# Tying the first feed-forward product of each token group behind attention in TensorE's queue

## The chip, the cores and the metric

The kernel runs on one core of a Trainium2 chip. The metric is the device time of one execution in microseconds (us). Its engines are TensorE (PE in the profile; PEld is its loading of weights), VectorE (DVE), ScalarE (ACT), GpSimd (POOL) and SyncE (SP, which issues the DMAs). Each engine works its own queue in order, and the queues run side by side, joined by semaphores.

## The reference

Attention, then two blocks of feed-forward layers, in fp32:

```python
# q, k, v: batch 2, heads 8, sequence 576, head size 64
q_d, k_d, v_d = mean over groups of 4 positions            # 144 positions
out_d = softmax(scale * q_d @ k_d.T) @ v_d                 # pooled attention
out_local = softmax(scale * q @ k.T where |i - j| < 4) @ v # local attention
x = repeat(out_d, 4) + out_local                           # 1152 tokens x 512
h = relu(x @ w_in); x = (s * h * h + b) @ w_out            # 512 -> 2048 -> 512
out = sum over 4 experts e of p[:, e] * (relu(x @ w1[e]) @ w2[e])   # 512 -> 1024 -> 512
```

## The kernel before

**Attention in units.** A unit is one head pair of one group of tokens. There are four groups (each of the two batch entries in two halves, of 256 and 320 tokens) with four head pairs each: 16 units, u = 0 to 15. A loop over `i` (line 979) runs a software pipeline. In iteration i it traces `b_step(i-1)` (scores: one mask product, the local score products of line 580, pooled products of line 594 or 604, then maxima on VectorE and exponentials on ScalarE), `a_step(i)` (transposes of k, line 487, for the first half of a batch entry, and of q, line 505), `k_step(i)`, `d_step(i-3)` (output products, lines 667 and 674), `c_step(i-2)` (transposes of the probabilities, line 646), `x_step(i-3)` (x of this head pair, split in a high and a low part), `norm_step(i-1)` and `v_step(i-1)`. For units 0 to 3 `keep_warm` (line 350) adds filler matmuls.

**The feed-forward products.** Each fp32 product is made of three reduced-precision ones (high times high, high times low, low times high, `PAIRS`), by the helper `products` (line 311; its matmuls are line 316). A product of the first layer contracts over four blocks of 128 rows, one for each head pair, so it is 12 matmuls, and the first three need x of head pair 0 only. The first feed-forward block (n = 0; 512 of the 2048 hidden columns) works on the attention's four token groups. For each group it has eight steps: four products of the first layer (`moe1_l1`, fc = 0 to 3; relu, square, scale and split of h behind each) and four of the second (`moe1_l2`). The weights come as halves of 256 columns, which ScalarE and VectorE reformat and split (`prep`, lines 154 to 203).

**The order.** When the last head pair of a group is done (`x_step` of u = 3, 7, 11, 15), the group's eight steps are appended to the list `slots` (line 1000). For group 0 three are taken at once; after that one is taken behind each `k_step` and each `c_step`, while there are any. So by the program the first product of group 0 stands behind `c_step(4)`, that of group 1 behind `a_step(11)` and that of group 2 behind `a_step(15)`. Group 3's steps are appended in the last iteration, and are taken in the loop of line 1018 and in the plan behind it.

This is the order of the trace, not that of the queues. The planner that makes the queues goes by the program's order as a priority, but puts an instruction ahead where, by its own estimates, the inputs are there and the engine would be free. A tile of a pool with a tag takes one of the tag's buffers when its first instruction is placed; the products' PSUM banks have the tag "m" with three buffers (pool `psm`), the attention's have five (pool `psa`).

After the attention (`actx.close()`, line 1021) all further blocks follow by a plan of due times.

Of the kernel before, what the change touches and what calls it, by code (L numbers as in the profile page):

```python
# [22 lines left out]
def attn_moe_moe_kernel(  # L23
# [14 lines left out]
    nc = tc.nc  # L38
# [11 lines left out]
    W = 72  # L50
# [6 lines left out]
    KD = DM // P  # L57
    BLK = 512
    FC = BLK // P
# [287 lines left out]
    idle = const.tile([P, 512], BF16, name="idle")  # L347
    nc.vector.memset(idle, 0.0)

    def keep_warm(ps, c0, m):  # L350
        for _ in range(m if c0 < 448 else 0):
            nc.tensor.matmul(  # L352
                ps[:, c0:], idle[:, :P], idle[:, : 512 - c0], start=True, stop=True
            )
# [122 lines left out]
    def a_step(u):  # L477
        g, j, b, hf = unit(u)
        if hf == 0:
            kn = loaded.pop(("k", u))  # L480
            kT = ap1.tile([P, S], F32, tag=f"kT{j}", name=f"kT{j}")
            view = kT.rearrange("p (n r) -> p n r", r=KR)
            m = KR // 2
            for c in range(2):
                psk = bank()
                for i in range(m):
                    nc.tensor.transpose(  # L487
                        psk[:, i * KP : i * KP + KP],
                        kn[:, c * m + i].rearrange("p a d -> p (a d)"),
                        ident[:KP, :KP],  # L490
                    )
                keep_warm(psk, m * KP, fill[u])
                nc.scalar.activation(
                    out=view[:, :, c * m : c * m + m],
                    in_=psk[:, : m * KP].rearrange("p (t n) -> p n t", n=KP),
                    func=ACTF.Copy,
                    scale=scale / (FAC * FAC),
                )
            st["kT", j] = kT
        qn = loaded.pop(("q", u))  # L500
        n0, m = tiles(hf)
        gd = m * TQ // FAC
        psq = bank()
        for r in range(FAC):
            nc.tensor.transpose(  # L505
                psq[:, r * gd : r * gd + gd],
                qn[:gd, r].rearrange("p a d -> p (a d)"),
                ident[:gd, :gd],
            )
        keep_warm(psq, m * TQ, fill[u])  # L510
        qz = ap2.tile([P, MX * TQ], F32, tag="qz", name="qz")[:, : m * TQ]
        nc.scalar.activation(
            out=qz.rearrange("p (t n r) -> p t n r", t=m, r=FAC),
            in_=psq[:, : m * TQ].rearrange("p (r t n) -> p t n r", r=FAC, t=m),
            func=ACTF.Copy,
            scale=float(FAC * FAC),
        )
        qd = ap2.tile([P, MX * TQ // FAC], F32, tag="qd", name="qd")[:, :gd]
        nc.vector.tensor_reduce(
            out=qd,  # L520
            in_=psq[:, : m * TQ].rearrange("p (r n) -> p n r", r=FAC),
            axis=AX.X,
            op=ALU.add,
        )
        st["q", u] = qz, qd
# [18 lines left out]
    def b_step(u):  # L544

        g, j, b, hf = unit(u)
        n0, m = tiles(hf)
        gd = m * TQ // FAC
        qz, qd = st.pop(("q", u))
        kT = st["kT", j]  # L550
        kd = st["kd", j]
        pl = ap2.tile([P, MX, W], F32, tag="pl", name="pl")[:, :m]
        ml = ap2.tile([P, MX, 1], F32, tag="ml", name="ml")[:, :m]
        both = gd == GB
        pd = ap2.tile([P, 2, SD], F32, tag="pd", name="pd")
        md = ap2.tile([P, 2, 1], F32, tag="md", name="md")
        if both:
            pd, md = pd[:, :1], md[:, :1]
        else:
            pd, md = pd[:gd], md[:gd]  # L560
        sm = sums[u % 2]

        def exps(out, ps, m, total):
            nc.scalar.activation(  # L564
                out=out, in_=ps, func=ACTF.Exp, bias=m, scale=1.0, accum_out=total
            )

        ps = [bank()] + ([] if both else [bank()])
        nc.tensor.matmul(  # L569
            ps[0][:, : m * W],  # L570
            identb.rearrange("p a q -> p (a q)"),
            mask[:, hf * 2 : hf * 2 + m].rearrange("p t w -> p (t w)"),
            start=True,
            stop=False,
        )
        for t in range(m):
            k0 = window(n0 + t)
            for a in range(2):
                o = slice(a * D, a * D + D)
                nc.tensor.matmul(  # L580
                    ps[0][a * TQ : a * TQ + TQ, t * W : t * W + W],
                    qz[o, t * TQ : t * TQ + TQ],
                    kT[o, k0 : k0 + W],
                    start=False,
                    stop=t == m - 1,
                )
        local = ps[0][:, : m * W].rearrange("p (t w) -> p t w", w=W)
        nc.vector.tensor_reduce(out=ml, in_=local, axis=AX.X, op=ALU.max, negate=True)
        pooled = [] if both else [ps[0][:gd, MX * W : MX * W + SD], ps[1][:gd, :SD]]
        if both:  # L590
            pooled = [ps[0][: 2 * gd, MX * W : MX * W + SD]]
            for a in range(2):
                o = slice(a * D, a * D + D)
                nc.tensor.matmul(  # L594
                    ps[0][a * gd : a * gd + gd, MX * W : MX * W + SD],
                    qd[o, :],
                    kd[o, :],
                    start=True,
                    stop=True,
                )  # L600
        else:
            for a in range(2):
                o = slice(a * D, a * D + D)
                nc.tensor.matmul(pooled[a], qd[o, :], kd[o, :], start=True, stop=True)  # L604
        for a in range(len(pooled)):
            nc.vector.tensor_reduce(
                out=md[:, a], in_=pooled[a], axis=AX.X, op=ALU.max, negate=True
            )
        for t in range(m):
            exps(pl[:, t], local[:, t], ml[:, t], sm[:, t])  # L610
        for a in range(len(pooled)):
            exps(pd[:, a], pooled[a], md[:, a], sm[: pd.shape[0], MX + a])
        st["p", u] = pl, pd
# [17 lines left out]
    def c_step(u):  # L631


        g, j, b, hf = unit(u)
        pl, pd = st.pop(("p", u))
        m, rows, n = pl.shape[1], pd.shape[0], pd.shape[1]
        pT = ap2.tile([W, (MX + MX // 2 + 1) * P], F32, tag="pT", name="pT")
        cols = [(pl[:, t], P) for t in range(m)]
        cols += [(pd[:, a, c * ND : c * ND + ND], rows) for a in range(n) for c in range(2)]
        c0 = 0  # L640
        while cols:
            ps = bank()
            n = 0
            while cols and n + cols[0][1] <= 512:
                x, width = cols.pop(0)
                nc.tensor.transpose(ps[:W, n : n + width], x, ident[:width, :width])  # L646
                n += width
            keep_warm(ps, n, fill[u])
            nc.scalar.copy(pT[:, c0 : c0 + n], ps[:W, :n])
            c0 += n  # L650
        st["pT", u] = pT

    def d_step(u):
# [8 lines left out]
        ps = bank()  # L662
        for a in range(2):
            o = slice(a * D, a * D + D)
            for c in range(2):
                i = m * P + ((c * 2 + a) if gd == GB else (a * 2 + c)) * gd
                nc.tensor.matmul(  # L667
                    ps[o, gq : gq + gd], vd[:, c, a], pT[:, i : i + gd], start=c == 0, stop=c == 1
                )
        for t in range(m):  # L670
            for a in range(2):
                o = slice(a * D, a * D + D)
                i = t * P + a * TQ
                nc.tensor.matmul(  # L674
                    ps[o, t * TQ : t * TQ + TQ],
                    vn[:, t, a],
                    pT[:, i : i + TQ],
                    start=True,
                    stop=True,
                )  # L680
# [298 lines left out]
    for i in range(last + 1):  # L979
# [13 lines left out]
        for f, lag in steps:  # L993
            u = i - lag
            if 0 <= u < NU:

                with tc.high_priority(30) if f is a_step and u < NP else nullcontext():
                    f(u)
            if f is x_step and u >= 0 and u % NP == NP - 1:
                slots += l1_steps(0, u // NP) + l2_steps(0, u // NP)  # L1000
                if u < NP:

                    for _ in range(3):
                        slots.pop(0)()
            if f in (k_step, c_step) and slots and i < last:
                slots.pop(0)()
            if f in (b_step, k_step, c_step, v_step):
                side_step()
        load_k(i + 2)
# [109 lines left out]
```

## Time and profile before

| | |
|---|---|
| Time, median of 3 runs | 699.72 us (697.83 to 700.53) |
| The profiled execution's own time | 702.75 us |
| Its span | 701.0 us |
| TensorE busy | 685.3 us (98%) |
| Weight loads busy | 617.2 us (88%) |
| VectorE, ScalarE, GpSimd busy | 404.9, 344.2, 102.6 us |
| Mean granted clock of TensorE | 0.974 of 2.4 GHz |

The times of rows are microseconds from the span's start. A granted clock of 1.00 is 2.4 GHz and 0.50 is 1.2 GHz; a value between says that both occurred in the stretch. "Idle before" is the time that the engine had nothing to work on, and behind the arrow stands what ended it. The attention runs until about 150 us; the rest of the span are the feed-forward blocks.

### The profile page before, as it was taken

How to read it: one execution, taken by the hardware profiler on the slowest of the kernel's cores; microseconds unless marked ns; L12 is line 12 of the kernel's file. 1: busy time of each engine (PE TensorE's matmuls, PEld its weight loads, DVE VectorE, ACT ScalarE, POOL GpSimd, SP SyncE). 2: the span in 40 equal slices, each digit the busy share in tenths (PEclk: the TensorE clock that was granted, in tenths of full speed). 3: DMA queues.
4: the chain of work that ended last, by engine and by line, in shares of the span. 5: the costliest groups of instructions: out<-in, count | busy, mean ns of one | idle time of the engine just before them, and what ended most of it. 6: DMA issues, size and time to landing. Idle time of an engine off the chain costs nothing.

```text
span 701.0 us, 11693 instructions
## 1 busy us (share of the span) xinstructions
PE 685.3 (98%) x4656; PEld 617.2 (88%) x4656; DVE 404.9 (58%) x720; ACT 344.2 (49%) x846; POOL 102.6 (15%) x123
## 2 busy tenths in 40 slices
PE   9979989999999999999999999999999999999997
PEld 5657868899999999999989898998998998998996
DVE  1577977779972533498344646645646456465442
ACT  3466857778875665765444423333334243233220
POOL 4230244010000200104021101201210112010000
PEclk8588999999999999999999999999999999999999
DMA  9465735413430000100111100301202102020012
GB/s 182 124 174 117 147 86 133 146 61 136 165 121 0 1 31 1 61 5 27 35 57 30 61 31 31 90 23 39 61 31 61 30 31 77 15 61 30 1 60 75
DMA packets 54166, 46.41 MB, mean 66 GB/s; under 512 B 32224, under 2 KB 42720, under 8 KB 54112
## 3 DMA queue, kind: packets, MB, share of 16 engines
q1 hardware_dynamic: 54112, 45.67, 23.6%
q8 instruction: 36, 0.59, 0.4%
q14 instruction: 18, 0.15, 0.1%
HBM read 43.31 MB, written 2.36 MB: 65 GB/s over the span
## 4 chain that ended last, share of the span: by engine, by line
PE 93%; DVE 3%; ACT 1%; issue 1%; POOL 1%; ACTq 0%; POOLq 0%
PE psm L316 43%; PE psx L852 25%; PE psx L316 13%; PE psa L352 2%; PE psa L580 2%; PE psa L646 2%; PE psa L674 1%; PE psa L487 1%; PE psa L667 1%; PE psa L505 1%; PE psa L604 1%; DVE pl L621 0%; PE psa L594 0%; PE psa L569 0%; ACT pl L564 0%
## 5 line engine op out<-in xcount | busy, mean ns | idle before, releaser
L316 PE MATMUL psm<-w,h 128*128 128x512 f32 x864 | 208.7, 391 | 0.0
L316 PEld LDWEIGHTS psm<-w,h 128*128 128x128 f32 x864 | 158.5, 188 | 30.0
L852 PE MATMUL psx<-x,w 128*128 128x320 f32 (+1 forms) x768 | 117.7, 296 | 0.0
L852 PEld LDWEIGHTS psx<-x,w 128*128 128x128 f32 x768 | 109.1, 189 | 1.7
L259 POOL TENSOR_TENSOR sw<-raw 128x256 f32<-128x256 f32 x32 | 30.9, 986 | 409.6 <-DMA raw<-in_moe_w_dram 269.8
L870 ACT ACTIVATE h<-r 128x320 fp32r<-128x320 f32 (+1 forms) x96 | 42.2, 444 | 84.9 <-DVE r L881 84.9
L867 ACT COPY r<-psx 128x320 f32<-128x320 f32 (+1 forms) x96 | 38.0, 396 | 92.2 <-PE psx L852 92.0
L852 PE MATMUL psx<-t,w 128*128 128x320 f32 (+1 forms) x448 | 80.2, 302 | 0.4 <-ACT r L867 0.4
L923 DVE SCALAR_TENSOR_TENSOR acc<-psm,pr,acc 128x512 f32<-128x512 f32 x63 | 47.2, 749 | 57.3 <-PE psm L316 57.3
L316 PE MATMUL psm<-x,w 128*128 128x320 f32 (+2 forms) x420 | 72.5, 319 | 6.1 <-ACT x L702 3.4
L881 DVE TENSOR_TENSOR r<-psx,r 128x320 f32<-128x320 f32 (+1 forms) x96 | 43.4, 457 | 59.3 <-PE psx L852 57.3
L316 PEld LDWEIGHTS psm<-x,w 128*128 128x128 f32 x420 | 64.6, 193 | 9.9 <-ACT x L702 4.2
L852 PEld LDWEIGHTS psx<-t,w 128*128 128x128 f32 x448 | 67.0, 188 | 4.6 <-ACT r L867 0.7
L871 DVE SCALAR_TENSOR_TENSOR h<-r,h 128x320 fp32r<-128x320 f32 (+1 forms) x96 | 48.4, 509 | 18.2 <-ACT h L870 16.1
L316 PE MATMUL psm<-h,w 128*128 128x256 f32 (+2 forms) x360 | 56.8, 306 | 0.8 <-ACT w L196 0.8
L316 PE MATMUL psx<-h,w 128*128 128x384 f32 (+1 forms) x312 | 55.8, 327 | 0.0
L316 PEld LDWEIGHTS psm<-h,w 128*128 128x128 f32 x360 | 50.7, 190 | 2.8 <-issue 1.3
L316 PEld LDWEIGHTS psx<-h,w 128*128 128x128 f32 x312 | 52.0, 188 | 0.0
L316 PE MATMUL psx<-x,w 128*128 128x384 f32 (+2 forms) x252 | 43.1, 320 | 0.0
L316 PEld LDWEIGHTS psx<-x,w 128*128 128x128 f32 x252 | 40.6, 188 | 0.0
L237 DVE TENSOR_TENSOR w<-raw,w 128x1024 fp32r<-128x1024 f32 x16 | 19.5, 1225 | 25.7 <-ACT w L234 25.7
L769 DVE TENSOR_TENSOR h<-r,h 128x384 fp32r<-128x384 f32 (+2 forms) x40 | 21.7, 541 | 20.1 <-ACT h L768 19.0
(103 smaller groups left out, 865.9 us busy)
## 6 DMA issues: line engine op xcount, KB each, us to landing
raw<-in_moe_w_dram SPq DMA_DIRECT2D x32, 512.0 KB
raw<-in_moe_w_in_dram SPq DMA_DIRECT2D x8, 1024.0 KB
raw<-in_moe_w_out_dram SPq DMA_DIRECT2D x8, 1024.0 KB
kn<-in_k_dram SPq DMA_DIRECT2D x8, 288.0 KB
v<-in_v_dram SPq DMA_DIRECT2D x8, 288.0 KB
out_dram<-acc SPq DMA_DIRECT2D x9, 256.0 KB
qn<-in_q_dram SPq DMA_DIRECT2D x8, 160.0 KB
vn<-in_v_dram SPq DMA_DIRECT2D x16, 72.0 KB
```

The costliest lines, as they stand in the source:

```text
L237: nc.vector.tensor_tensor(out=k0[1], in0=source(), in1=f32(k0[0]), op=ALU.subtract)
L259: nc.gpsimd.tensor_tensor(out=operand(out), in0=operand(x), in1=operand(y), op=op)
L316: nc.tensor.matmul(o, stat(ps, kk), mov(pm, kk, i), start=c == 0, stop=c == len(terms) - 1)
L352: nc.tensor.matmul(ps[:, c0:], idle[:, :P], idle[:, : 512 - c0], start=True, stop=True)
L580: nc.tensor.matmul(ps[0][a * TQ : a * TQ + TQ, t * W : t * W + W], qz[o, t * TQ : t * TQ + TQ], kT[o, k0 : k0 + W], start=False, stop=t == ...
L769: nc.vector.tensor_tensor(out=h[1], in0=r, in1=f32(h[0]), op=ALU.subtract)
L852: nc.tensor.matmul(ps, s_ap(n, half, a, w, kk), xt[x, pi][b][:, kk], start=first and c == 0, stop=c == len(terms) - 1, skip_group_check=True,)
L867: nc.scalar.copy(t, st[name])
L870: nc.scalar.activation(out=h[0][:, halves[hf]], in_=t, func=ACTF.Relu)
L871: nc.vector.scalar_tensor_tensor(out=h[1][:, halves[hf]], in0=t, scalar=0.0, in1=f32(h[0][:, halves[hf]]), op0=ALU.max, op1=ALU.subtract,)
L881: nc.vector.tensor_tensor(out=st[t], in0=st[name], in1=st[t], op=ALU.add)
L923: nc.vector.scalar_tensor_tensor(out=a, in0=ps, scalar=p_e, in1=a, op0=ALU.mult, op1=ALU.add)
```

## The change

The kernel records the last attention matmul that was traced (`last_pe["att"]`), at every transpose and product of `a_step`, `b_step`, `c_step` and `d_step`; the filler matmuls are not recorded. It keeps a list of the first products of the groups (`firsts`: the eighth step from the end of `slots` at the time of appending, `moe1_l1` with fc = 0). Steps are taken in the attention loop by a helper; for a step in `firsts` the helper opens `tc.issue_after` on the recorded matmul. That adds, for each TensorE instruction traced in the block, an edge to the recorded one: it is queued behind it on TensorE. It is an order of issue only and adds no wait for a result. Nothing else that the step issues (ScalarE, VectorE) gets an edge. The loop of line 1018 and the plan do not use the helper.

```diff
+    last_pe = {}
+    firsts = []
+
+    def take_slot():
+        f = slots.pop(0)
+        with tc.issue_after(last_pe["att"].ins) if f in firsts else nullcontext():
+            f()
...
-                    nc.tensor.transpose(
+                    last_pe["att"] = nc.tensor.transpose(
                         psk[:, i * KP : i * KP + KP],
...
-                nc.tensor.matmul(pooled[a], qd[o, :], kd[o, :], start=True, stop=True)
+                last_pe["att"] = nc.tensor.matmul(pooled[a], qd[o, :], kd[o, :], start=True, stop=True)
...
-                nc.tensor.transpose(ps[:W, n : n + width], x, ident[:width, :width])
+                last_pe["att"] = nc.tensor.transpose(ps[:W, n : n + width], x, ident[:width, :width])
...
             if f is x_step and u >= 0 and u % NP == NP - 1:
                 slots += l1_steps(0, u // NP) + l2_steps(0, u // NP)
+                firsts.append(slots[-FC - KD])
                 if u < NP:
 
                     for _ in range(3):
-                        slots.pop(0)()
+                        take_slot()
             if f in (k_step, c_step) and slots and i < last:
-                slots.pop(0)()
+                take_slot()
```

## Rows read from the trace of the kernel before

**Rows 1.** Windows: stretch, length, busy us of each engine (instructions), TensorE's clock, DMA.
```profile
20.00:30.00 10.00, 8.71 (x51) 5.29 (x51) 4.84 (x12) 3.80 (x14) 2.70 (x4) 0.50 0.58 161
...
36.00:46.00 10.00, 7.54 (x96) 5.29 (x94) 6.37 (x12) 5.22 (x19) 3.35 (x4) 1.00 0.67 179
46.00:58.00 12.00, 10.27 (x78) 7.96 (x78) 9.57 (x19) 7.15 (x22) 3.56 (x4) 0.57 0.54 127
58.00:66.00 8.00, 7.19 (x83) 5.53 (x82) 5.53 (x18) 4.45 (x21) 0.00 (x0) 1.00 0.89 197
...
84.00:101.00 17.00, 14.00 (x166) 11.36 (x167) 14.19 (x25) 9.45 (x36) 8.00 (x9) 1.00 0.53 96
101.00:106.00 5.00, 5.00 (x27) 4.39 (x28) 3.12 (x8) 3.44 (x15) 1.20 (x3) 0.66 0.35 92
106.00:150.00 44.00, 43.99 (x539) 37.59 (x537) 32.43 (x72) 33.15 (x122) 10.30 (x10) 1.00 0.47 135
```

**Rows 2.** Timeline of TensorE, 37 to 69 us: start, duration, instruction, [idle before].
```profile
37.09 0.50 PE L316 MATMUL psm<-x,w 128*128 128x256 f32 x2
37.98 0.74 PE L316 MATMUL psm<-x,w 128*128 128x256 f32 x4 [0.38 <-POOL x L704]
38.65 0.46 PE L594 MATMUL psa<-kd,qd 64*64 64x144 f32 x4
...
45.43 0.38 PE L316 MATMUL psm<-x,w 128*128 128x256 f32 x1 [1.43 <-ACT x L702]
46.71 0.94 PE L316 MATMUL psm<-x,w 128*128 128x256 f32 x5 [0.90 <-POOL x L704]
47.58 0.77 PE L604 MATMUL psa<-kd,qd 64*80 64x144 f32 x2
...
50.09 1.22 PE L316 MATMUL psm<-x,w 128*128 128x256 f32 x4 [1.02 <-DVE w L199]
51.11 0.73 PE L505 MATMUL psa<-ident,qn 80*128 80x80 f32 x4
...
56.15 0.48 PE L569 MATMUL psa<-mask,identb 64*128 64x360 bf16 x1
...
58.20 1.35 PE L316 MATMUL psm<-x,w 128*128 128x256 f32 x9
...
62.52 0.32 PE L569 MATMUL psa<-mask,identb 64*128 64x360 bf16 x1
...
65.20 3.26 PE L316 MATMUL psm<-x,w 128*128 128x256 f32 x20 [0.48 <-ACT x L702]
```

**Rows 3.** Timeline of VectorE and ScalarE: a maximum and a first exponential.
```profile
39.16 0.31 DVE L606 TENSOR_REDUCE md<-psa 128x1 f32<-128x144 f32 x1 [1.45 <-PE psa L594]
...
48.78 0.32 ACT L564 ACTIVATE pl<-psa,ml 128x72 f32<-128x72 f32 x1 [1.63 <-DVE md L606]
```

**Rows 4.** Timeline of TensorE, 129 to 135 us.
```profile
129.10 0.74 PE L316 MATMUL psm<-x,w 128*128 128x256 f32 x4
...
130.63 0.44 PE L505 MATMUL psa<-ident,qn 80*128 80x80 f32 x4
...
133.46 1.68 PE L316 MATMUL psm<-x,w 128*128 128x256 f32 x12
```

**Rows 5.** Timeline of TensorE: sixteen local score products at the low and the high clock.
```profile
27.14 1.22 PE L580 MATMUL psa<-kT,qz 64*64 64x72 f32 x16
...
98.00 0.72 PE L580 MATMUL psa<-kT,qz 64*64 64x72 f32 x16
```

**Rows 6.** Groups by line, TensorE, 84 to 106 us: group and count | busy, mean ns.
```profile
L316 PE MATMUL psm<-x,w 128*128 128x320 f32 x43 | 9.1, 355 | 1.8 <-ACT x L702 1.5 <-POOL x L704 0.3
```

**Rows 7.** Timeline of TensorE, 84 to 106 us.
```profile
84.65 2.22 PE L316 MATMUL psm<-x,w 128*128 128x320 f32 x14
...
94.38 0.46 PE L594 MATMUL psa<-kd,qd 64*64 64x144 f32 x4 [0.84 <-DVE ml L588]
...
101.35 1.74 PE L316 MATMUL psm<-x,w 128*128 128x320 f32 x7
...
105.80 0.46 PE L505 MATMUL psa<-ident,qn 64*128 64x64 f32 x4
```

More of the change, by code (lines that the diff above doesn't have):

```diff
@@ L504, in a_step @@
         for r in range(FAC):
-            nc.tensor.transpose(
+            last_pe["att"] = nc.tensor.transpose(
                 psq[:, r * gd : r * gd + gd],
@@ L568, in b_step @@
         ps = [bank()] + ([] if both else [bank()])
-        nc.tensor.matmul(
+        last_pe["att"] = nc.tensor.matmul(
             ps[0][:, : m * W],
@@ L579, in b_step @@
                 o = slice(a * D, a * D + D)
-                nc.tensor.matmul(
+                last_pe["att"] = nc.tensor.matmul(
                     ps[0][a * TQ : a * TQ + TQ, t * W : t * W + W],
@@ L593, in b_step @@
                 o = slice(a * D, a * D + D)
-                nc.tensor.matmul(
+                last_pe["att"] = nc.tensor.matmul(
                     ps[0][a * gd : a * gd + gd, MX * W : MX * W + SD],
@@ L666, in d_step @@
                 i = m * P + ((c * 2 + a) if gd == GB else (a * 2 + c)) * gd
-                nc.tensor.matmul(
+                last_pe["att"] = nc.tensor.matmul(
                     ps[o, gq : gq + gd], vd[:, c, a], pT[:, i : i + gd], start=c == 0, stop=c == 1
@@ L673, in d_step @@
                 i = t * P + a * TQ
-                nc.tensor.matmul(
+                last_pe["att"] = nc.tensor.matmul(
                     ps[o, t * TQ : t * TQ + TQ],
```

## Prediction

> **What bounds the kernel now.** I read the windows first, then TensorE's order of work with the other engines' rows beside it. From 106 to 150 us TensorE is busy 43.99 of 44.00 us [rows 1], and behind the attention come feed-forward products alone: from about 106 us the kernel is bound by TensorE, and what TensorE does not get done earlier is paid there one for one. Before that it has holes and a slower clock: 2.46 us idle in 36 to 46, 1.73 us idle and a granted clock of 0.57 in 46 to 58, 3.00 us idle in 84 to 101, a clock of 0.66 in 101 to 106 [rows 1]. So the change is worth what it takes from, or adds to, idle time and slow clock before 106 us; the matmuls are the same in number.
>
> TensorE works its queue in order. The queue order shows that the first feed-forward products of group 0 run far ahead of their place in the program. Their place is behind the transposes of `c_step(4)`, but 27 of them (three products, a quarter of the contraction at a time, as each head pair's x appears) stand between 37.09 and 58.20: 2, 4, 1, 5, 2 (a pair at 48.27, not shown), 4 and 9 [rows 2]. The last quarter follows when x of pair 3 is there, at 65.20. Three of these early products wait at the head of the queue: 1.43 us for x from ScalarE, 0.90 us for x from GpSimd, 1.02 us for a weight half from VectorE [rows 2].
>
> **Group 0: what goes.** The three PSUM banks tagged "m" are handed out in program order, so with the first product tied behind `c_step(4)` the second and third, which are not tied themselves, cannot take a bank earlier either. All 27 leave the stretch from 37 to 59 us.
>
> (1) The pooled scores of unit 3 no longer stand behind six products: 37.15 instead of 38.65 [rows 2]. VectorE's maximum waited 1.45 us for them [rows 3], so the exponentials of unit 3 begin about 1.45 us earlier.
> (2) The second pooled product of unit 4 moves from 47.58 to about 42.5. Its maximum does not follow by as much: VectorE is busy 9.57 of 12 us in 46 to 58 [rows 1], and the row sums, the mask scores' maximum and the normalization of unit 3 come before it in its queue. The exponentials of unit 4, at 48.78 now after 1.63 us of waiting for that maximum [rows 3], gain about 1.4 us, not 5.
> (3) What stands behind the products on TensorE, `a_step(5)`, `d_step(2)`, `c_step(3)` (51.11 to 56.1), then fits before about 47.5. So `b_step(5)` starts when the exponentials of unit 4 give its bank back, near 51.0, instead of at 56.15 [rows 2]: 5.1 us earlier. For x of pair 3 VectorE's queue is then the bound: between 46 and 66 us it has 2.43 + 2.47 = 4.9 us idle to give [rows 1]. I take 4.5: the last quarter could start at 60.7 instead of 65.20.
> (4) The 27 products must still be done. Twelve of this shape took 1.68 us [rows 4], 0.14 us each, 3.8 us in all. `c_step(4)` would end near 56.0; until 60.7 there are 4.7 us, of which `b_step(6)` takes 2.2 us (from 62.52 to the idle 0.48 us before 65.20 now) [rows 2]. So 2.5 us of them are hidden by the wait for x of pair 3, and 1.3 us are on the path. Gain 4.5 - 1.3 = 3.2 us.
> (5) The clock. TensorE would idle from about 47.5 to 51. In 46 to 58, behind such waits, the granted clock was 0.57 [rows 1], and sixteen score products took 1.22 us at 1.2 GHz against 0.72 us at 2.4 GHz [rows 5], 1.7 times. About one unit of attention, 4.7 us (worked out below), then stands in the slow stretch; 3.3 us more, of which most lies beside VectorE's work. I take 0.6 us. Group 0: -2.6 us.
>
> Bounds: if all idle time of 36 to 58 (4.2 us) and the whole cost of the slow clock there (10.27 us busy, 86% of it at half clock, 41% of that lost: 3.6 us) went, -7.8 us; if x of pair 3 came only the 1.4 us of step (2) earlier, the 1.3 us of (4) eat it: 0.
>
> **Group 1: what is taken away.** Its first product is popped behind `a_step(11)`, whose transposes of q stand at 105.80. Now 43 products of the group run before that, from 84.65 on [rows 6]: 29 before 101.35, and fourteen from there, in two runs of seven (one shown) with the transposes of k between [rows 7]. The 29 took TensorE time that attention could not use: the pooled scores of unit 9 waited 0.84 us for VectorE's maximum, not for a product, and VectorE is busy 14.19 of 17 us in this stretch [rows 1, 7]. So I take the attention up to 101 us to last as long without the products, and TensorE's idle time to rise from 3.0 by 29 x 0.159 = 4.6 us (fourteen took 2.22 us from 84.65); TensorE's 14.00 busy us less these are 4.7 us of attention for each of the stretch's two units. What is saved is at the end: the fourteen products between 101.35 and 105.80 no longer stand before `a_step(11)`. Its transposes of q can start between 99.5 (drawn into the gap in which `b_step(10)` waits for its maximum, its pooled products, 0.4 us, then still to do) and 102.1 (behind them and the transposes of k). The 43 products are 6.8 us, so the loss is 99.5 + 0.4 + 6.8 - 105.8 = 0.9 to 102.1 + 6.8 - 105.8 = 3.1 us; the middle is 2.0. The clock adds: in 20 to 30 us, attention with its filler matmuls alone, the clock was 0.50, and it was 0.66 in 101 to 106, behind the stretch with 3.00 us idle [rows 1]. If it stays low until the products return, `a_step(11)` and the first 3 us of them lose up to 3 us; much of the rest is hidden behind VectorE, as before. I take 0.6. Group 1: +2.6 us, between +0.5 and +6.1.
>
> **Groups 2 and 3.** The first product of group 2 is popped behind `a_step(15)`. Only seven products stand before its transposes now (129.10 to 130.63) [rows 4], and TensorE has no idle time there: they change places, 0 to +0.5 us, taken as 0. Group 3 is popped in the loop after the attention, which does not use the new helper: 0. The edges are of order only: no DMA, no queue of SyncE or GpSimd, and no semaphore is touched. ScalarE's and VectorE's work on h moves with its products into stretches where both have room (33.15 and 32.43 of 44 us) [rows 1].
>
> **The sum.** -2.6 + 2.6 + 0 = 0.0 us on the profiled execution's own 702.75 us, which is 0.4% above the median of 699.72 us; so 699.7 us on the scale of the medians.
>
> The rows give 0.14 and 0.159 us for each product. The Trainium skill (TensorE: Matmul & The Clock Gate, Back-to-back issue gap) states for isolated products at full clock the columns over 2.4 GHz plus 2.5 ns. By that, an estimate, 0.109 and 0.136 us would be put back: 0.8 us less on the path in group 0, 1.0 us less in group 1, and 697.9 us. The rows here are longer than the rule, so the sum goes by the rows.
>
> **Rivals.** *Faster: the waits were the whole of it.* With nothing at the queue's head that waits for x, TensorE keeps its clock through 46 to 58, and `a_step(11)` is drawn ahead as far as banks allow. For it: the 3.35 us of waits on early products and the slow clock begin together. Against it: VectorE's load. Group 0 -5.5 us (of at most 7.8), group 1 +0.4: 694.6 us.
>
> *Slower: attention alone does not hold the clock.* In group 1's hole of some 16 to 20 us TensorE has only small attention products and no filler (the filler matmuls exist for units 0 to 3 alone). From the point where the granted clock falls to 1.2 GHz, near 86 us, 4.7 us of attention per unit cost 8.0 us, more than VectorE's 7.1, so TensorE becomes the chain, and the first products start slow: group 1 +6.1. The same happens near 50 us, and group 0 keeps -0.8: 705.0 us. For it: 0.50 in 20 to 30 us [rows 1]. Against it: the clock of 1.00 in 84 to 101, with idle time there too.
>
> *It does not do what it says.* If a later product may take a bank before an earlier one, the second, third and fourth products of a group run ahead in the place of the first, with the same waits, and the first comes last: up to +0.5 us for the later start of the second layer, 700.0 us.
>
> **How the numbers follow.** Changes below 0.5%, 3.5 us, cannot be told from none here. Forecast (699.7, its own range 697 to 702.5): 0.40, of which 0.34 within 0.5% and 0.03 on either side. Faster rival: 0.33, of which 0.30 beyond 0.5%. Slower rival: 0.19, of which 0.18 beyond. No effect: 0.08. So faster 0.33, same 0.46, slower 0.21. The range from 694.0 to 704.5 takes in most of both outer cases.
>
> **What would show it.** Group 0: no feed-forward product before `c_step(4)`'s transposes; the second pooled product of unit 4 near 42.5; `b_step(5)` near 51; x of pair 3 near 60. If `b_step(5)` stays at 55 or later, step (3) is wrong. Group 1: no product between the end of group 0's second layer and `a_step(11)`, which itself should stand 3 to 6 us earlier; idle time there of 7 us or more, and the granted clock of this stretch decides between forecast and slower rival. If `a_step(11)` comes more than 7 us earlier, the products did hold attention up there and I am wrong towards faster. If products stand in either stretch, the third rival holds.

## The result, and the profile after

The change makes the kernel slower by about 1%: a median of 709.13 us (705.84 to 711.56, four runs) against 700.12 us for the kernel before (697.83 to 702.96, four runs). The ratio is 1.0113 with a 95% interval of 1.007 to 1.0156. The profiled execution took 711.56 us, its span is 709.8 us, 8.8 us longer than before, and TensorE's mean granted clock is 0.959 against 0.974.

The lines of the code after are eight higher (the transposes of q are L513, of k L495, of the probabilities L654; local scores L588, pooled products L602 and L612, maxima L596 and L614, exponentials L572, x L710), while the products stay at L316.

The windows of the kernel after, over the stretches of [rows 1] (columns as there):

```profile
36.00:46.00 10.00, 6.53 (x93) 4.75 (x91) 7.19 (x15) 5.85 (x22) 3.70 (x4) 1.00 0.77 190
46.00:58.00 12.00, 10.38 (x93) 7.37 (x95) 11.07 (x21) 7.88 (x26) 3.80 (x4) 0.57 0.70 162
58.00:66.00 8.00, 8.00 (x70) 7.41 (x69) 4.41 (x13) 5.00 (x19) 0.00 (x0) 0.80 0.71 150
84.00:101.00 17.00, 12.32 (x134) 9.45 (x132) 13.23 (x23) 9.49 (x36) 9.55 (x10) 0.63 0.49 89
101.00:106.00 5.00, 4.51 (x22) 3.82 (x23) 2.60 (x8) 2.61 (x13) 0.79 (x2) 0.50 0.46 117
106.00:150.00 44.00, 43.42 (x464) 36.77 (x464) 29.20 (x63) 28.83 (x108) 7.75 (x9) 0.93 0.44 132
```

Read the clock (third number from the right) against [rows 1]. From 36 to 58 us it is what it was, 1.00 and 0.57; in 58 to 66 it is 0.80 instead of 1.00. From 84 to 101 it has fallen from 1.00 to 0.63, from 101 to 106 from 0.66 to 0.50, and even the stretch behind, where TensorE is busy 43.42 of 44.00 us, is at 0.93.

Where the time went is dated by one mark: group 1's second layer ends with a run of twelve products, which in the kernel before stands here on TensorE's timeline:

```profile
125.73 2.01 PE L316 MATMUL psm<-h,w 128*128 128x320 f32 x12
```

In the kernel after, TensorE's timeline from the end of group 0 to that mark:

```profile
83.74 0.76 PE L316 MATMUL psm<-h,w 128*128 128x256 f32 x5
84.34 0.66 PE L495 MATMUL psa<-ident,kn 96*128 96x96 f32 x6
84.93 0.46 PE L513 MATMUL psa<-ident,qn 64*128 64x64 f32 x4
85.32 0.51 PE L675 MATMUL psa<-pT,vd 72*64 72x80 f32 x8
...
94.23 0.74 PE L602 MATMUL psa<-kd,qd 64*64 64x144 f32 x4 [3.43 <-DVE ml L596]
...
99.61 1.22 PE L588 MATMUL psa<-kT,qz 64*64 64x72 f32 x16
101.49 0.74 PE L602 MATMUL psa<-kd,qd 64*64 64x144 f32 x4 [0.65 <-DVE ml L596]
...
103.31 0.69 PE L513 MATMUL psa<-ident,qn 64*128 64x64 f32 x4
103.92 3.57 PE L316 MATMUL psm<-x,w 128*128 128x320 f32 x12
107.42 0.70 PE L675 MATMUL psa<-pT,vd 72*64 72x64 f32 x8
...
110.06 3.06 PE L316 MATMUL psm<-x,w 128*128 128x320 f32 x12
113.05 0.29 PE L577 MATMUL psa<-mask,identb 64*128 64x288 bf16 x1
...
113.93 0.49 PE L513 MATMUL psa<-ident,qn 80*128 80x80 f32 x4
114.22 0.83 PE L316 MATMUL psm<-x,w 128*128 128x320 f32 x4
...
116.74 0.46 PE L675 MATMUL psa<-pT,vd 72*64 72x64 f32 x8
...
118.20 2.00 PE L316 MATMUL psm<-x,w 128*128 128x320 f32 x12
120.13 0.32 PE L577 MATMUL psa<-mask,identb 64*128 64x360 bf16 x1
...
134.78 2.01 PE L316 MATMUL psm<-h,w 128*128 128x320 f32 x12
```

Group 0 ends at 84.34, where its end was at 84.65 [rows 7]: 0.3 us gained. The mark stands at 134.78 instead of 125.73, 9.05 us later. So the whole loss of this execution arises in group 1, between 84 and 135 us. As the change says, no product of the group stands between 84.34 and 103.92. The local scores take 1.22 us, which is their time at 1.2 GHz [rows 5].

The loss in its parts:

- **Order.** 43 products that stood before `a_step(11)` [rows 6] now stand behind it: 6.8 us, an estimate at 0.159 us each. It comes 105.80 - 103.31 = 2.5 us earlier for that [rows 7]. 6.8 - 2.5 = 4.3 us lost.
- **Clock, behind `a_step(11)`.** There TensorE is the bound but still at 1.2 GHz. The 12 products from 103.92 last until 107.42 and the 12 from 110.06 until 113.05: 6.49 us for 24. At full clock twelve last from 118.20 to 120.13, 1.93 us, so 24 would last 3.86: 2.6 us lost. The same attention instructions between two such runs take 2.64 us (107.42 to 110.06) against 1.46 (116.74 to 118.20): 1.2 us. The transposes of q take 0.61 (103.31 to 103.92) against 0.39 for the same shape at full clock (84.93 to 85.32): 0.2 us. Together 4.0 us.
- 9.05 - 4.3 - 4.0 leaves some 0.7 us; 0.58 us of it is a new wait for a maximum that ends at 122.8 (not shown).

How long the clock was low is seen in finer windows of the kernel after:

```profile
84.00:88.50 4.50, 3.41 (x53) 2.98 (x51) 4.50 (x8) 3.96 (x17) 0.95 (x2) 1.00 0.96 178
88.50:94.00 5.50, 2.30 (x22) 1.65 (x21) 5.50 (x8) 1.80 (x4) 5.07 (x5) 0.50 0.19 18
94.00:104.00 10.00, 9.12 (x76) 6.65 (x76) 4.27 (x11) 5.05 (x25) 3.53 (x5) 0.50 0.46 106
103.90:112.20 8.30, 8.30 (x51) 7.68 (x51) 3.38 (x8) 3.65 (x12) 1.99 (x4) 0.50 0.10 22
113.00:120.00 7.00, 7.00 (x80) 6.02 (x79) 4.48 (x12) 5.05 (x19) 1.05 (x3) 1.00 0.45 111
```

It is at 0.50 from 88.5 to 112.2. In the first 5.5 us of that VectorE is busy all the time, so the low clock costs nothing there; from 94 on TensorE is busy 9.12 of 10.00 us, and from 103.9 all the time, and it costs.

The three largest waits of TensorE in the kernel after, from 36 to 125 us (tile and line, what it waited for: us, times, longest):

```profile
PE psa L602 <- DVE ml L596: 4.8, 3, 3.4
PE psa L612 <- DVE ml L596: 3.2, 2, 2.6
PE psa L654 <- ACT pd L572: 2.4, 2, 1.3
```

The three waits of early products for x and a weight half [rows 2] are gone. In their place attention's own instructions wait for VectorE's maxima and ScalarE's exponentials: in group 1 the products had filled waits that were there anyway: the pooled products of unit 9 still come at 94.23, where they came at 94.38 [rows 7].

Group 0, TensorE's timeline of the kernel after, beside [rows 2]:

```profile
38.38 0.46 PE L602 MATMUL psa<-kd,qd 64*64 64x144 f32 x4 [0.75 <-DVE ml L596]
...
46.34 0.47 PE L612 MATMUL psa<-kd,qd 64*80 64x144 f32 x2 [2.64 <-DVE ml L596]
...
51.32 0.64 PE L654 MATMUL psa<-ident,pd 128*72 128x128 f32 x2 [1.28 <-ACT pd L572]
...
52.75 0.48 PE L577 MATMUL psa<-mask,identb 64*128 64x360 bf16 x1
...
60.22 0.74 PE L654 MATMUL psa<-ident,pd 80*72 80x80 f32 x4
60.70 4.78 PE L316 MATMUL psm<-x,w 128*128 128x256 f32 x36
```

and ScalarE's, beside [rows 3]:

```profile
48.29 0.32 ACT L572 ACTIVATE pl<-psa,ml 128x72 f32<-128x72 f32 x1 [1.43 <-DVE md L614]
...
61.43 0.40 ACT L710 CAST x<-xg 128x256 fp32r<-128x256 f32 x1
```

`b_step(5)` does come 3.4 us earlier (52.75, not 56.15), and x of pair 3 some 3 us. But all 36 matmuls of the first three products then stand in one run of 4.78 us behind `c_step(4)`, and x of pair 3 is there (cast at 61.43) before the run needs it: nothing of what was taken out is hidden.

### The profile page after: what moved, and what is told of

It is laid out like the page before. It is cut to its first block, busy times and chain, and to the rows that moved or that the text cites. A ratio compares the mean times of both kernels' runs of the same rounds, so it can differ in the third digit from the quotient of the medians.

```text
span 709.8 us, 11700 instructions
## 1 busy us (share of the span) xinstructions
PE 691.5 (97%) x4656; PEld 623.0 (88%) x4656; DVE 406.3 (57%) x720; ACT 345.6 (49%) x846; POOL 102.9 (14%) x123
## 4 chain that ended last, share of the span: by engine, by line
PE 92%; DVE 5%; ACT 1%; issue 1%; DMA 1%; ACTq 0%
PE psm L316 42%; PE psx L860 25%; PE psx L316 13%; PE psa L588 2%; PE psa L654 2%; PE psa L360 1%; PE psa L682 1%; PE psa L513 1%; PE psa L612 1%; PE psa L495 1%; PE psa L675 1%; DMA kn<-in_k_dram 1%; PE psa L602 1%; PE psa L577 1%; DVE cv L186 0%
## 5 line engine op out<-in xcount | busy, mean ns | idle before, releaser
L316 PE MATMUL psm<-w,h 128*128 128x512 f32 x864 | 208.7, 391 | 0.0
L316 PEld LDWEIGHTS psm<-w,h 128*128 128x128 f32 x864 | 158.5, 188 | 30.1
L316 PE MATMUL psm<-x,w 128*128 128x320 f32 (+2 forms) x420 | 70.8, 320 | 0.0
L316 PEld LDWEIGHTS psm<-x,w 128*128 128x128 f32 x420 | 65.4, 197 | 1.3 <-issue 1.1
L316 PE MATMUL psm<-h,w 128*128 128x256 f32 (+2 forms) x360 | 56.5, 305 | 0.0
L316 PE MATMUL psx<-h,w 128*128 128x384 f32 (+1 forms) x312 | 55.9, 327 | 0.0
L316 PEld LDWEIGHTS psx<-h,w 128*128 128x128 f32 x312 | 52.0, 188 | 0.0
L316 PEld LDWEIGHTS psm<-h,w 128*128 128x128 f32 x360 | 50.8, 190 | 1.3 <-issue 0.8
L316 PE MATMUL psx<-x,w 128*128 128x384 f32 (+2 forms) x252 | 43.1, 320 | 0.0
L316 PEld LDWEIGHTS psx<-x,w 128*128 128x128 f32 x252 | 40.6, 188 | 0.0
```

Source lines behind the costliest of these rows:

```text
L316: nc.tensor.matmul(o, stat(ps, kk), mov(pm, kk, i), start=c == 0, stop=c == len(terms) - 1)
```

## The experiments

**Which group.** Four kernels ran beside the kernel before (700.96 us, 29 runs; the first series): two tie one group alone, two add filler matmuls.

Group 0 alone:

```diff
-                firsts.append(slots[-FC - KD])
+                if u < NP:
+                    firsts.append(slots[-FC - KD])
```

> Only group 0's first product is tied; groups 1 and 2 run as before. Theory A (the loss is group 1's: its products leave a stretch in which TensorE is idle anyway, and the clock falls there): group 0's tie is worth nothing, since the second layer of group 0 ended at 84.34 us with the change and at 84.65 without; this run takes 700 us, within 1.5 of the kernel before. Rival B (every tied group costs its share, about 4.5 us for each of groups 0 and 1): 704 to 705 us. Rival C (group 0's tie gains 3 us, as I forecast, and group 1 loses 12): 697 us.

Measured: 701.29 us, ratio 1.0013 (0.9984 to 1.0042). The tie of group 0 is worth nothing that can be measured (-1.1 to +2.9 us by the interval): neither the gain of 2.6 us that the forecast gave it nor a loss of 4 us.

Group 1 alone (`if u // NP == 1:` in the same place):

> Only group 1's first product is tied. Theory A: the whole loss, 709 us, and the same trace from 84 us on: no feed-forward product between about 84 and 103 us, granted clock 0.50 from about 89 to 112 us. Rival B: 704 to 705 us. Rival C: 712 us.

Measured: 709.29 us, ratio 1.011 (1.0064 to 1.0157): the whole loss. TensorE's windows of that kernel repeat those of the kernel after:

```profile
84.00:101.00 17.00, 12.31 (x129) 9.68 (x130) 13.54 (x23) 9.44 (x36) 7.95 (x8) 0.62 0.48 97
101.00:106.00 5.00, 4.35 (x29) 3.44 (x27) 2.16 (x8) 2.58 (x13) 0.88 (x3) 0.50 0.36 89
```

**Order or clock.** The kernel after with 60 filler matmuls in `a_step(9)` to `a_step(11)` and `c_step(8)`, which are meant to hold the clock and leave the order of TensorE's other work as it is:

```diff
+    fill_a = [6 if 9 <= u < 12 else fill[u] for u in range(NU)]
+    fill_c = [6 if u == 8 else fill[u] for u in range(NU)]
...
-                keep_warm(psk, m * KP, fill[u])
+                keep_warm(psk, m * KP, fill_a[u])
...
-        keep_warm(psq, m * TQ, fill[u])
+        keep_warm(psq, m * TQ, fill_a[u])
...
-            keep_warm(ps, n, fill[u])
+            keep_warm(ps, n, fill_c[u])
```

> The changed kernel with filler matmuls (six behind each bank of transposes of a_step 9, 10 and 11 and of c_step 8, 60 in all, some 6 us of TensorE), put into the stretch that the tie empties. Theory A, in two terms: 4.3 us because 43 products come after a_step(11), which itself comes only 2.5 us earlier, and some 4 us because the clock stays at 1.2 GHz until 112 us while TensorE is the bound. If the filler holds the clock at 2.4 GHz, the second term goes and the first stays: 704 to 706 us. Rival D (the order alone costs it all; the clock costs nothing because VectorE is the bound): 709 us or, with the filler in the way, up to 712.

Measured: 706.28 us, ratio 1.0058 (1.0023 to 1.0094). Its windows, and on TensorE's timeline the end of group 0, the first products behind `a_step(11)` and the mark:

```profile
84.00:101.00 17.00, 14.21 (x173) 10.96 (x171) 10.95 (x24) 9.21 (x37) 8.38 (x9) 0.90 0.45 88
101.00:106.00 5.00, 5.00 (x60) 4.43 (x59) 2.32 (x6) 2.96 (x15) 1.12 (x2) 1.00 0.43 104
```

```profile
82.87 0.41 PE L497 MATMUL psa<-ident,kn 96*128 96x96 f32 x3
...
102.04 0.46 PE L515 MATMUL psa<-ident,qn 64*128 64x64 f32 x4
...
103.01 2.01 PE L316 MATMUL psm<-x,w 128*128 128x320 f32 x12
...
130.43 2.01 PE L316 MATMUL psm<-h,w 128*128 128x320 f32 x12
```

The clock is back (0.90 and 1.00; over all runs the mean granted clock is 0.979, as in the kernel before with 0.979, against 0.967 for group 1 alone), and the twelve products take 2.01 us. The time comes back by 3.0 us only (709.29 to 706.28, same series), near the 4.0 us read from the rows; 0.6% stays lost at full clock, near the 4.3 us of order. The halves are rough, but neither is nothing: the means of the runs, 708.74 us (six) and 705.54 us (twelve), are 3.2 us apart with a 95% interval of 0.4 to 6.0, and the interval of what stays lost excludes 1. The traces say where the time came back. From the end of group 0 to `a_step(11)` it takes 19.2 us with the fillers (82.87 to 102.04) and 19.0 without (84.34 to 103.31): nothing gained. From there to the mark it takes 28.4 us instead of 31.5: 3.1 us, where the clock was low and is not.

The same 60 fillers in the kernel before:

> The kernel before with the same 60 filler matmuls. It tells what the filler itself costs or gives where products stand in the stretch: TensorE has 3.0 us idle there and 3.3 us at 1.2 GHz. Theory A: some of the 6 us fit into the idle time and the low clock from 102 to 105 us goes (1.4 us back): 700 to 704 us. Rival D: 6 us more less 3 us of idle time, 703 us and more, with no gain from the clock.

Measured: 701.08 us, ratio 1.0001 (0.9972 to 1.0031). There the fillers neither cost nor bring anything that can be measured (what they cost and what they bring were not told apart), so what they brought above they brought in the stretch that the tie had emptied.

**How much is held back.** In a second series, beside the kernel before (701.4 us, 33 runs), group 1's first product is tied behind `a_step(10)` instead of `a_step(11)`:

```diff
+    marks = {}
...
-        with tc.issue_after(last_pe["att"].ins) if f in firsts else nullcontext():
+        mark = marks[10] if f in firsts[1:2] else last_pe.get("att")
+        with tc.issue_after(mark.ins) if f in firsts else nullcontext():
...
+                if f is a_step:
+                    marks[u] = last_pe["att"]
```

> The changed kernel with group 1's first product tied behind a_step(10) instead of a_step(11), one unit earlier. Theory A: the price is the TensorE time without products, so it falls with the length of that stretch. The products can start near 96 us instead of 103.9, the idle time of 96 to 103 is used, the idle 4.3 us between 86 and 94 and the low clock that follows them stay: 703 to 706 us. Rival F (the price is not the stretch's length but that the group runs in program order at all): 708 to 709 us.

Measured: 705.11 us, ratio 1.006 (1.0035 to 1.0085), about half the loss. TensorE's timeline and windows of it (this execution took 702.1 us, one of the faster of twelve):

```profile
96.69 1.97 PE L316 MATMUL psm<-x,w 128*128 128x320 f32 x6
...
103.12 0.46 PE L515 MATMUL psa<-ident,qn 64*128 64x64 f32 x4
```

```profile
84.00:101.00 17.00, 12.70 (x108) 9.71 (x106) 10.29 (x19) 7.07 (x32) 8.73 (x9) 0.70 0.35 77
101.00:106.00 5.00, 5.00 (x69) 4.27 (x67) 3.90 (x10) 4.13 (x14) 1.22 (x2) 1.00 0.16 35
```

The products return at 96.69, still at the slow clock, and from 101 on it is full. With the first product tied one unit earlier the loss is smaller, as it should be if it grows with the time for which the products are held out. The mean clock over its runs is 0.971, between 0.967 (group 1 alone) and 0.977 (the kernel before in that series).

Group 2 alone (`if u // NP == 2:`):

> Only group 2's first product is tied, behind a_step(15). Theory A: seven products change places with one set of transposes in a stretch where TensorE has no idle time: 700 to 701 us, within 1.5 of the kernel before. Rival E (also there the tie delays the elementwise work on h and the second layer): 702.5 us or more.

Measured: 700.57 us, ratio 1.0003 (0.9979 to 1.0028): nothing that can be measured.

**What holds the other products.** One edge ties one product, and yet all products of the group leave the hole. In a third series (kernel before: 700.03 us, 23 runs) the kernel after gives the tied product of group 1 a bank of the attention's pool:

```diff
-        ps = mm_bank()[:, :m]
+        ps = (bank() if n == 0 and g == 1 and fc == 0 else mm_bank())[:, :m]
```

> The changed kernel, with one difference: group 1's first product takes its PSUM bank from the attention's pool instead of from the three banks of the feed-forward products. It is tied behind a_step(11) as before, but it no longer stands first in the order in which those three banks are handed out. Theory A (the tie holds back the whole group only through the order of the banks, and the price is the empty stretch): the second to fourth product, 36 matmuls, stand in 84 to 103 us again, the clock stays high there, and the 12 of the first come behind a_step(11): 700 to 702.5 us. Rival G (the price is the tied product itself, whose h the second layer needs first): 706 us or more.

Measured: 701.39 us, ratio 1.0012 (0.9978 to 1.0046). TensorE's timeline of it:

```profile
83.31 1.78 PE L316 MATMUL psm<-x,w 128*128 128x320 f32 x11
...
98.65 0.74 PE L316 MATMUL psm<-x,w 128*128 128x320 f32 x2 [1.32 <-ACT x L710]
...
102.86 0.46 PE L513 MATMUL psa<-ident,qn 64*128 64x64 f32 x4
103.25 2.02 PE L316 MATMUL psa<-x,w 128*128 128x320 f32 x12
```

The tied product still stands behind `a_step(11)` (in `psa`, at 103.25), but the others are back in the hole from 83.31 on, with their wait of 1.32 us for x, and the loss is gone within the interval (up to 3.2 us). So it is the order of the three banks by which one edge holds the whole group, and products that wait at the head of the queue bring no loss that can be measured here. The execution shown took 705.84 us, one of three near 706 among the twelve runs; behind 106 us its clock falls once more (0.92 in 106 to 150), which wasn't followed up.

**What the waits of group 0 are worth.** If waits and low clock are the kernel's loss from 36 to 58 us, TensorE should be kept busy there, not emptied. Thirty filler matmuls stand before the pooled products of unit 4, with the tie of group 0 and without it (the kernel before with the filler alone):

```diff
+        for _ in range(30 if u == 4 else 0):
+            nc.tensor.matmul(
+                ps[0][:, MX * W : MX * W + SD], idle[:, :P], idle[:, :SD], start=True, stop=True
+            )
```

> Group 0's first product tied alone, and 30 filler matmuls of 144 columns (about 2 us) between the local and the pooled scores of unit 4, where TensorE waited 2.64 us for VectorE in the changed kernel. If the low clock of 46 to 58 us is what ate group 0's gain, and this wait brings it: clock above 0.8 in 46 to 58, and 697 to 699 us. If VectorE's queue sets the pace of the units there, clock or not: 700 to 702 us.

> The kernel before with the same 30 filler matmuls. Here the products wait for x behind them. If the filler holds the clock, 698 to 700 us, about 1 to 2 us behind the one with group 0 tied; if VectorE sets the pace, 700 to 702 us like that one.

Measured, in the second series: 696.95 us with the tie, ratio 0.9945 (0.9924 to 0.9967), and 696.5 us without it, 0.9942 (0.9916 to 0.9968). The filler is worth some 0.55%, more than I expected without the tie; the 1 to 2 us that I expected of the tie beside it did not come, and with the tie the clock in 46 to 58 is 0.72, not above 0.8. Both kernels with the filler beat the kernel before and the kernel after. The windows of the kernel before with the filler:

```profile
36.00:46.00 10.00, 9.29 (x93) 7.33 (x94) 6.11 (x13) 5.43 (x17) 4.20 (x5) 0.66 0.67 159
46.00:58.00 12.00, 10.92 (x136) 8.74 (x133) 10.20 (x20) 7.39 (x28) 4.16 (x3) 1.00 0.65 180
```

The low clock is not gone in this execution, it lies earlier, in 36 to 46. Over all runs the mean granted clock is 0.984 in both kernels with the filler, against 0.977 for the kernel before. A share of (1 - clock) x 2 of the span at half clock makes 32 us of 700 before and 22 us with it: 10 us less. By [rows 5] half clock loses 41% of a busy stretch, 4.1 us of 10, and 4.9 us were gained (701.4 to 696.5; 4.1 by the ratio). That fits the clock as the cause; that it is the whole of it wasn't shown.

A second filler, twenty matmuls in unit 10, on top (third series):

```diff
+        for _ in range({4: 30, 10: 20}.get(u, 0)):
```

> The kernel before, without any tie, with the filler in unit 4 of the run before last (30 matmuls) and 20 more at the same place in unit 10, before the stretch from 102 to 105 us in which its clock was low. If the low clock there costs its 1.4 us: 695 to 696 us, 0.6 to 0.8% below the kernel before. If the filler's 1.3 us are on the path, since products could have run there: 697 to 698 us.

Measured: 697.07 us, ratio 0.996 (0.9929 to 0.9991), no more than the first alone; the intervals overlap.

## Why the prediction was wrong

The mechanism that decided was on the list, as the slower rival; the forecast said no change, and the time lies above its range.

**What held.** With the first product tied, the second and third cannot take a bank: all leave both stretches, and giving the tied one another bank brings those of group 1 back. Group 2's tie is worth nothing that can be measured (1.0003), and group 3's first product is not tied. The loss in group 1 was told as order plus clock, with `a_step(11)` earlier and the granted clock deciding.

**Group 1, the clock term.** This is the step that failed most: I took 0.6 us, and it is 4.0. I argued from the clock of 1.00 in 84 to 101 [rows 1] that attention with idle time keeps its clock. But the products that the change removes were a part of what TensorE did in that stretch. The row that answered was the other one that I quoted, 20 to 30 us, attention with fillers at 0.50 [rows 1]. The rival had the sign but was too cheap as well: it put +6.1 on group 1, and 9.05 came. It let the clock return with the first 3 us of products, a length that no row gave; the clock stayed at 0.50 for 8.3 us of full TensorE work, from 103.9 to 112.2.

**Group 1, the order term.** I took 2.0 us, from `a_step(11)` between 99.5 and 102.1; it is 4.3, with `a_step(11)` at 103.31. Two figures of this sum were loose: the lower end of +0.5 lies below the 0.9 that the sum gives, and the fourteen products behind the 0.159 us are followed by the next instruction after 2.06 us (at 86.71, not shown), 0.147 each, by which 43 are 6.3 us and not 6.8. The premise that VectorE sets attention's pace held at first: the pooled products of unit 9 stand at 94.23, after 94.38 before. Behind it, at half clock, TensorE's own attention work did not fit: 9.12 busy of 10.00 us from 94 to 104, and idle time in 84 to 101 is 4.7 us, not the 7.6 that I drew. So part of what I count as order may be the slow clock under another name. The fillers do not show it: with them `a_step(11)` comes as long after the end of group 0 as without (19.2 and 19.0 us), but they take TensorE's time there themselves, and the remaining loss of 0.6% carries them too.

**Group 0, -2.6 us.** Step (1) gave 0.27 us, not 1.45: the pooled scores of unit 3 stand at 38.38, now waiting 0.75 us for VectorE. Step (2) failed at its root: the second pooled product of unit 4 stands at 46.34, not 42.5, because it waits 2.64 us for the maximum of the local scores on VectorE, where I had let it run as soon as the products were out of its way; the exponentials gained 0.49 us, not 1.4. Step (3) then came to 52.75 instead of 51.0. Step (4) had `c_step(4)` end near 56.0 and hide 2.5 us of the 27 products; it ended at 60.96 (60.22 + 0.74), so nothing was hidden. Step (5), the clock, was too small: it did not move in 46 to 58, but in 58 to 66 it fell from 1.00 to 0.80. From `b_step(5)` to the run of 36 attention takes 7.95 us (52.75 to 60.70), with TensorE busy throughout; before, it took 5.2 (56.15 to 62.52 [rows 2], less nine products at 0.133 us, 36 in 4.78): 2.8 us lost, where I took 0.6. Of the 3.4 us by which `b_step(5)` is earlier little is left, and group 0 alone measures 1.0013. This low clock goes with the tie: in 58 to 66 it is 0.79 to 0.95 in all five executions with group 0 tied and no filler in unit 4, and 1.00 in all six without the tie (windows not shown).

**The other rivals.** The faster one, that the waits were the whole of it, is out: the waits at the queue's head went (3.35 us by my count; [rows 2] shows a fourth, of 0.38 us, that I left out), and group 0 alone is not faster; they came back in group 1 with the other bank, at no measurable loss. That the change does nothing is out, since no product stands in either stretch.

**The rule cited.** The Trainium skill (TensorE: Matmul & The Clock Gate, Back-to-back issue gap) gives, for isolated products at full clock, the columns over 2.4 GHz plus 2.5 ns: an estimate of 0.136 us at 320 columns. The trace does not agree: twelve take 1.93 us, 0.161 each, with a weight load to each. The sum went by the rows, and rightly, though this was not what decided.

## What to carry to other kernels

Before work is taken out of an engine's waits, ask what the engine does there without it: products that run ahead can use time that is lost otherwise, even when they wait at the queue's head, and what is held back is paid where the engine is the bound. The granted clock of a stretch belongs to the work that is in it; when the change removes part of that work, read the clock from a stretch that already lacks it. And an order edge on the first user of a small pool of buffers can tie all that follow in the pool.

## What the runs showed of the hardware

Once at 0.50, in the kernel after, TensorE's granted clock stayed there through 8.30 us in which TensorE was busy without a break with products of 320 columns and some attention, and was 1.00 in the window from 113.

A higher mean clock is not a shorter time by itself. Sixty filler matmuls with which the mean clock rose from 0.979 to 0.983 brought no time (1.0001), thirty with which it rose from 0.977 to 0.984 brought 0.6% (0.9942). The fillers take TensorE's time too: with the sixty it is busy 17.00 of 17.00 us from 84 to 101. And from 88.5 to 94.0 us in the kernel after a clock of 0.50 cost nothing, with VectorE busy throughout.

Where the clock is low differs between executions of nearly the same work. The kernel with group 0 alone tied has a clock of 0.66 in 36 to 46, where the kernel after, which ties group 0 in the same way, has 1.00:

```profile
36.00:46.00 10.00, 9.36 (x99) 7.11 (x99) 7.19 (x14) 5.54 (x17) 5.16 (x6) 0.66 0.70 153
```

So the clock of one profile up to 58 us is that execution's: the readings of 36 to 58 us above hold for the executions shown, and between kernels the means over runs were compared.
